# Four weight blocks of an attention-plus-MLP kernel, loaded and split in another place

## The chip, the cores and the metric

The kernel runs on one core of a Trainium2 chip. The metric is the device time of one execution in microseconds, the median of several runs. The core's engines are TensorE (PE, matmuls into the accumulators, PSUM), VectorE (DVE), ScalarE (ACT), GpSimd (POOL) and SyncE (SP), which here issues nearly all the DMA transfers. Each engine takes its instructions strictly in the order in which the program has them, and waits where one of them needs data or a buffer that isn't there.

## The reference

Causal attention with a decay bias over 4 batches of 8 heads, 576 positions and 64 dimensions per head, and behind it two MLPs over the 2304 tokens (512 to 2048 to 512), the first with a leaky ReLU, the second with a softplus.

```
scores = scale * q @ k.T
cum = cumsum(max(s, 0))
scores = where(causal, -1e9, scores + min(-(cum_i - cum_j), 0))
attn = exp(scores - max) / (sum + 1e-9)
x = (attn @ v) rearranged to [2304, 512]
x = leaky(x @ w_in) @ w_out          # first MLP
out = softplus(x @ w2_in) @ w2_out   # second MLP
```

## The kernel before

**Number format.** The matmuls of the MLPs get their operands as pairs of a high and a low part; a product is three matmuls (high by high, high by low, low by high). The weights come from memory in 64-bit words, so each block (512 KB, either an "i" block of w_in or an "o" block of w_out for 128 hidden units) is loaded raw by `load_w` (lines 86 to 96) and then split by `split_w` (98 to 134): two reads of the raw buffer on ScalarE (L105, L106), three steps on VectorE (`clamp` L111, `shift` L114, `sign` L117), an `add` on GpSimd (L120), `high` on ScalarE (L124, which writes wih or woh) and `low` on GpSimd (L130, which writes wil or wol). The two reads are written down at once; the other six steps are put off with `later` by a number of ticks that the call gives (`at`), and `tick` writes down what is due. The order in which the Python code writes the instructions down is the order on each engine: there is no scheduler behind it. A raw buffer is free again when `sign` has read it.

**Attention.** 16 pairs of heads (`NP`), each of four score units, so 64 steps of the loop in `attention` and three more that drain it (step n 0 to 66). The score and transpose matmuls of a step are interleaved with ScalarE's exponentials, VectorE's maxima and GpSimd's scaling (L306). A step has two ticks.

**Units of the first MLP beside it.** A batch that the attention has finished (`ready`) gives 16 units for the first group of four hidden blocks (`G` = 4): an h unit (`Fill.h`) is twelve matmuls of 288 columns and then, each a tick later, gf (ScalarE, L518), gh (ScalarE, L523) and gl (GpSimd, L528); an o unit (`Fill.o`) is twelve matmuls that use the gh and gl of four h units, three for each, in the order gh, gl, gh, and then a copy on ScalarE (L543) and a store of 144 KB on SyncE (L544). `Fill.run` takes one unit per step. Its accumulators rotate over five banks at the end.

**The loads.** `Fill.step` starts a block's load at the steps in `self.loads`, through the single rawi buffer and two rawo buffers, and its split three steps later: the first group's eight blocks from steps 0 to 25, and then four blocks of the second group (4i, 4o, 5i, 5o) at steps 30, 35, 40 and 45, into tiles of a second weight pool with two buffers (`wpool2`).

**Leftover units and main loop.** When the attention is done, seven units are left, three h and four o; a loop runs one of them and a tick per turn (lines 558 to 560). In two turns of it no unit is ready, since the o units need the last gl; TensorE has nothing between, so its order is h, h, h, o, o, o, o. Then come new raw buffers, the loads of the stored part results into `acc` (L567), and the main loop: per step twelve h matmuls (L143), act1 (L605 and others), and the out matmuls (L651) of three steps before. Its `plan` loads and splits the second group's other blocks and all later ones.

Of the kernel before, what the change touches and what calls it, by code (L numbers as in the profile page):

```python
# [19 lines left out]
G = 4  # L20
# [10 lines left out]
def attn_moe_moe(ctx, tc, q, k, v, s, w1i, w1o, w2i, w2o, out):  # L31
# [18 lines left out]
    def pool(name, bufs=1, **kw):  # L50
        return tc.tile_pool(name=name, bufs=bufs, **kw)
# [14 lines left out]
    def later(n, fn, *args):  # L66
        todo.setdefault(clock[0] + n, []).append((fn, args))

    def tick():
        clock[0] += 1  # L70
        for fn, args in todo.pop(clock[0], ()):
            fn(*args)
# [7 lines left out]


    wt, wio = {}, {}
    wpools = [ctx.enter_context(pool(f"wpool{n}", bufs=n)) for n in (G, 2)]
    wio["tmp"] = ctx.enter_context(pool("wtmp", bufs=2))

    def load_w(layer, f, nm, place=None):
        w = ((w1i, w1o), (w2i, w2o))[layer]["io".index(nm)].bitcast(I32)
        raw = (place or wio[nm]).tile([P, 2 * DM], I32, tag="raw", name="raw" + nm)
        if nm == "i":
            nc.sync.dma_start(  # L90
                raw.rearrange("p (k f) -> p k f", k=KD),
                w[:, 2 * f * P:2 * (f + 1) * P].rearrange("(k p) f -> p k f", p=P),
            )
        else:
            nc.sync.dma_start(raw, w[f * P:(f + 1) * P, :])
        wt[layer, f, nm, "raw"] = raw.rearrange("p (e t) -> p e t", t=2)

    def split_w(layer, f, nm, at):

        raw = wt.pop((layer, f, nm, "raw"))  # L100
        L, Hw = raw[:, :, 0], raw[:, :, 1]
        m = wio["tmp"].tile([P, DM], I32, tag="wm", name="wm")
        t = wio["tmp"].tile([P, DM], I32, tag="wt", name="wt")
        wp = wpools[0 if (layer * NF + f) % 6 < 4 else 1]
        nc.scalar.activation(m.bitcast(F32), Hw.bitcast(F32), AF.Abs)  # L105
        nc.scalar.activation(t, L.bitcast(U32), AF.Copy, scale=2.0 ** -29)  # L106

        mf = m.bitcast(F32)

        def clamp():  # L110
            nc.vector.tensor_scalar(mf, mf, D_MIN, D_MAX, op0=ALU.max, op1=ALU.min)  # L111

        def shift():
            nc.vector.tensor_scalar(m, m, 3, 0x3FFFFFFF, op0=ALU.logical_shift_left, op1=ALU.bitwise_and)  # L114

        def sign():
            nc.vector.scalar_tensor_tensor(m, Hw, -0x40000000, m, op0=ALU.bitwise_and, op1=ALU.bitwise_or)  # L117

        def add():
            nc.gpsimd.tensor_tensor(m, m, t, op=ALU.add)  # L120

        def high():
            hi = wp.tile([P, DM], F32R, tag=f"w{nm}h", name=f"w{nm}h")
            nc.scalar.activation(hi, m.bitcast(F32), AF.Copy)  # L124
            wt[layer, f, nm] = [hi]

        def low():
            lo = wp.tile([P, DM], F32R, tag=f"w{nm}l", name=f"w{nm}l")
            hi = wt[layer, f, nm][0]
            nc.gpsimd.tensor_tensor(lo, m.bitcast(F32), hi.bitcast(F32), op=ALU.subtract)  # L130
            wt[layer, f, nm].append(lo)

        for n, fn in zip(at, (clamp, shift, sign, add, high, low)):
            later(n, fn)
# [317 lines left out]
    class Fill:  # L452
        def __init__(self, ps):
            self.ps = ps
            self.units = []
            new = lambda nm, bufs=1: self.stack.enter_context(pool(nm, bufs, side="right"))
            self.stack = ExitStack()
            wio["i"] = new("rawi")
            with_o = pool("rawo", 2, side="right")
            wio["o"] = with_o.__enter__()  # L460

            blocks = [(f, nm) for nm in "io" for f in range(G)] + [(G + f, nm) for f in range(2) for nm in "io"]
            self.loads = dict(zip((0, 2, 5, 8, 11, 15, 20, 25, 30, 35, 40, 45), zip(blocks, "ioooo" + "i" * 7)))

            def begin():

                with_o.__exit__(None, None, None)
                self.gpool, self.tpool = new("gpoolA", G + 1), new("tpoolA", 2)

            self.begin = begin  # L470
# [77 lines left out]
    with pool("psA", bufs=2, space=PSUM) as psA:  # L548
        fills = []

        def make():
            fills.append(Fill(psA))
            return fills[0]

        with pool("att") as att:
            attention(att, psA, make)
        fill = fills[0]
        while fill.units or todo:
            fill.run()
            tick()  # L560
        fill.stack.close()

    for nm in "io":
        wio[nm] = ctx.enter_context(pool("raw" + nm))
    acc = ctx.enter_context(pool("accpool")).tile([P, KD, NT], F32, tag="acc", name="acc")
    for c in range(2 * (B - 1)):
        nc.sync.dma_start(acc[:, :, c * CW:(c + 1) * CW], part[c])  # L567
# [106 lines left out]
    for gi, (layer, g) in enumerate(groups[1:]):  # L674
        a, z = start[groups[gi]], start[layer, g]
        when = [a + 2, a + 5, a + 8, a + 11, z - 3, z, z - 1, z + 2]
        for j, n in enumerate(when):
            if gi == 0 and j < 4:
                continue
            f, nm = divmod(j, 2)  # L680
            w = (layer, g * G + f, "io"[nm])
# [65 lines left out]
```

## Time and profile before

| | |
|---|---|
| runs | 1022.63, 1022.64 and 1021.40 us, median 1022.63 |
| profiled execution | 1022.12 us, of it 1020.20 us span from the first to the last instruction |
| busy, share of the span | PE 97%, DVE 50%, ACT 53%, POOL 55% |
| TensorE's granted clock | 0.997 of 2.4 GHz as a mean |
| stretch with the four splits and the rest of the attention, 112.82 to 263.10 | PE busy 149.55 of 150.28 us |
| leftover units, 263.10 to 275.90 | PE 11.72, ACT 4.63, POOL 2.40, DVE 0.00 us busy of 12.80 |
| first MLP from there, 275.90 to 628.00 | PE busy 349.54 of 352.10 us |
| second MLP, 628.00 to 1020.20 | PE busy 382.67 of 392.20 us |

Times in the rows count from the span's start. "Busy" adds up the durations of an engine's instructions without counting overlap twice. A row of the timeline gives, in brackets, how long the engine was idle before it and what ended that wait.

### The profile page before, as it was taken

The page shows a single profiled execution, that of the slowest core. Times are in us where ns is not written, and L with a number is a line of the kernel's source. Part 1 is how long each engine was busy: PE and PEld are TensorE (multiplying, and loading weights), DVE is VectorE, ACT ScalarE, POOL GpSimd, SP SyncE. Part 2 cuts the span into 40 slices and gives each one's busy share as a digit, 9 for nine tenths or more (in the row PEclk, how much of TensorE's full clock was granted, in tenths as well). Part 3 has the DMA queues.
Part 4 walks back from the last instruction along what each step waited for, and adds up shares of the span by engine and source line. Part 5 has one row for each costly group of instructions (what it writes and reads, how often), then busy time and mean ns, then how long its engine had stood idle before and what let it go on. Part 6 is the DMA issues. An engine that isn't in the chain of part 4 may idle for free.

```text
span 1020.2 us, 15105 instructions
## 1 busy us (share of the span) xinstructions
PE 992.0 (97%) x5498; PEld 812.4 (80%) x5498; DVE 506.3 (50%) x1133; ACT 536.8 (53%) x1152; POOL 559.2 (55%) x565
## 2 busy tenths in 40 slices
PE   7889999999999999999999998999999999999998
PEld 4667788888998888888888887888778877888886
DVE  6886665554021312321244158547575767576443
ACT  4877676656355333432444365666645554565452
POOL 6757455434156335533553356667766676667453
PEclk9999999999999999999999999999999999999999
DMA  5422333210252002100220021101210121010202
GB/s 172 135 97 67 113 106 101 93 59 25 73 205 76 22 1 83 63 21 1 83 62 22 16 68 41 42 2 45 80 42 1 42 82 42 1 42 21 83 22 83
DMA packets 38518, 62.04 MB, mean 61 GB/s; under 512 B 2932, under 2 KB 25972, under 8 KB 38444
## 3 DMA queue, kind: packets, MB, share of 16 engines
q1 hardware_dynamic: 38204, 60.74, 18.2%
q8 instruction: 44, 0.72, 0.3%
q10 hardware_dynamic: 240, 0.33, 0.1%
q14 instruction: 30, 0.25, 0.1%
HBM read 52.65 MB, written 8.40 MB: 60 GB/s over the span
## 4 chain that ended last, share of the span: by engine, by line
PE 73%; POOL 10%; DVE 8%; issue 6%; ACT 3%; DMA 0%; DVEq 0%; POOLq 0%; ACTq 0%
PE ps_h L143 30%; PE ps_out L651 27%; PE pt_v L354 4%; PE ps_o L539 4%; PE pt_s L262 4%; POOL t L619 3%; PE pt_t L323 3%; POOL gl L150 2%; POOL wm L120 2%; DVE wm L114 2%; PE pt_s L252 2%; ACT sc L295 1%; DVE wm L111 1%; DVE wm L117 1%; POOL wil L130 1%
## 5 line engine op out<-in xcount | busy, mean ns | idle before, releaser
L150 POOL TENSOR_TENSOR gl<-gf,gh 128x512 fp32r<-128x512 f32 (+2 forms) x148 | 178.3, 1206 | 258.9 <-ACT gh L149 243.4
L143 PE MATMUL ps_h<-xh,wih 128*128 128x512 f32 (+2 forms) x688 | 246.5, 358 | 1.1 <-ACT o L543 0.6
L143 PE MATMUL ps_h<-xl,wih 128*128 128x512 f32 (+2 forms) x688 | 244.7, 356 | 0.0
L143 PE MATMUL ps_h<-xh,wil 128*128 128x512 f32 (+2 forms) x688 | 243.9, 354 | 0.0
L143 PEld LDWEIGHTS ps_h<-xh,wih 128*128 128x128 f32 x688 | 129.4, 188 | 21.5 <-ACT o L543 0.8
L306 POOL TENSOR_SCALAR sc<-sc,st 128x512 f32<-128x512 f32 (+4 forms) x160 | 88.1, 562 | 103.8 <-DVE st L302 61.3
L143 PEld LDWEIGHTS ps_h<-xl,wih 128*128 128x128 f32 x688 | 129.4, 188 | 19.0
L143 PEld LDWEIGHTS ps_h<-xh,wil 128*128 128x128 f32 x688 | 129.4, 188 | 18.5
L662 DVE TENSOR_TENSOR acc<-ps_out,acc 128x512 f32<-128x512 f32 (+1 forms) x114 | 67.7, 655 | 129.1 <-PE ps_out L651 129.1
L149 ACT ACTIVATE gh<-gf 128x512 fp32r<-128x512 f32 (+2 forms) x148 | 85.3, 576 | 82.7 <-DVE gf L624 81.8
L605 ACT ACTIVATE gf<-ps_h 128x512 f32<-128x512 f32 (+2 forms) x68 | 36.7, 539 | 172.1 <-PE ps_h L143 168.2
L651 PE MATMUL ps_out<-woh,gh 128*128 128x512 f32 x288 | 116.2, 403 | 5.8 <-ACT gh L149 3.2
L624 DVE TENSOR_TENSOR gf<-gf,t 128x512 f32<-128x512 f32 (+1 forms) x80 | 56.0, 700 | 127.0 <-POOL t L619 127.0
L111 DVE TENSOR_SCALAR wm<-wm 128x512 f32<-128x512 f32 x64 | 42.1, 658 | 147.3 <-ACT wm L105 140.3
L651 PE MATMUL ps_out<-wol,gh 128*128 128x512 f32 x288 | 115.0, 399 | 0.0
L295 ACT ACTIVATE sc<-sc,st 128x512 f32<-128x512 f32 (+2 forms) x144 | 83.3, 581 | 42.9 <-DVE st L286 22.0
L120 POOL TENSOR_TENSOR wm<-wm,wt 128x512 int32<-128x512 int32 x64 | 88.1, 1377 | 28.0 <-DVE wm L117 28.0
L619 POOL TENSOR_TENSOR t<-e,t 128x512 f32<-128x512 f32 (+1 forms) x80 | 98.3, 1228 | 0.0
L651 PE MATMUL ps_out<-gh,woh 128*128 128x512 f32 (+2 forms) x272 | 97.1, 365 | 0.0
L651 PE MATMUL ps_out<-gh,wol 128*128 128x512 f32 (+2 forms) x272 | 96.6, 364 | 0.0
L281 DVE CUSTOM_DVE_ANT_0 sc<-pt_s,mask 128x512 f32<-128x512 f32 (+2 forms) x144 | 66.7, 480 | 57.2 <-PE pt_t L323 46.1
L651 PE MATMUL ps_out<-woh,gl 128*128 128x512 f32 x288 | 80.6, 397 | 1.2 <-POOL gl L150 1.1
(93 smaller groups left out, 1729.2 us busy)
## 6 DMA issues: line engine op xcount, KB each, us to landing
rawi<-in_moe_w_in SPq DMA_DIRECT2D x32, 512.0 KB
rawo<-in_moe_w_out SPq DMA_DIRECT2D x32, 512.0 KB
V<-in_v SPq DMA_DIRECT2D x16, 320.0 KB
Q<-in_q SPq DMA_DIRECT2D x15, 320.0 KB
K<-in_k SPq DMA_DIRECT2D x16, 288.0 KB
out<-acc SPq DMA_DIRECT2D x18, 256.0 KB
part<-o SPq DMA_DIRECT2D x24, 144.0 KB
acc<-part SPq DMA_DIRECT2D x6, 576.0 KB
```

The source lines that it names most:

```text
L111: nc.vector.tensor_scalar(mf, mf, D_MIN, D_MAX, op0=ALU.max, op1=ALU.min)
L120: nc.gpsimd.tensor_tensor(m, m, t, op=ALU.add)
L143: nc.tensor.matmul(ps, a, b, start=n == 0, stop=n == 3 * KD - 1)
L149: nc.scalar.activation(gh, gf, AF.Copy)
L150: nc.gpsimd.tensor_tensor(gl, gf, gh.bitcast(F32), op=ALU.subtract)
L281: nc.vector.tensor_tensor_reduce(out=self.sc[:, j, c], in0=self.ps[j][:, c], in1=m, scale=-scale, scalar=3.0e38, op0=ALU.add, op1=ALU.min, ...
L295: nc.scalar.activation(x, x, AF.Exp, scale=-1.0, bias=self.stat(0, e), accum_out=self.stat(1, e))
L306: nc.gpsimd.tensor_scalar(x, x, self.stat(2, e), 1.0, op0=ALU.mult, op1=ALU.mult)
L619: nc.gpsimd.tensor_tensor(t, e, t, op=ALU.subtract)
L624: nc.vector.tensor_tensor(gf, gf, t, op=ALU.add)
L651: nc.tensor.matmul(ps, a, b, start=f == 0 and m == 0, stop=f == G - 1 and m == 2)
L662: nc.vector.tensor_tensor(d, o, d, op=ALU.add)
```

## The change

The four blocks 4i, 4o, 5i and 5o leave the list of the attention. The pool for their split tiles and one raw buffer each for i and o blocks are opened only when the attention's tiles have been given up, so they take that room. The loop over the leftover units now loads 4i and 4o in its turn 0, before that turn's unit, and 5i and 5o in turn 5; it writes the reads of 4i down in turn 2, of 4o in turn 3, of 5i in turn 7 and of 5o in turn 8, and the other six steps of a split 1, 1, 2, 2, 3 and 4 ticks later instead of 1 to 6.

```diff
-    wpools = [ctx.enter_context(pool(f"wpool{n}", bufs=n)) for n in (G, 2)]
+    wpools = [ctx.enter_context(pool("wpool", bufs=G))]
...
-            blocks = [(f, nm) for nm in "io" for f in range(G)] + [(G + f, nm) for f in range(2) for nm in "io"]
-            self.loads = dict(zip((0, 2, 5, 8, 11, 15, 20, 25, 30, 35, 40, 45), zip(blocks, "ioooo" + "i" * 7)))
+            blocks = [(f, nm) for nm in "io" for f in range(G)]
+            self.loads = dict(zip((0, 2, 5, 8, 11, 15, 20, 25), zip(blocks, "ioooo" + "i" * 3)))
...
+        wpools.append(ctx.enter_context(pool("wpool2", bufs=2)))
+        for nm in "io":
+            wio[nm] = ctx.enter_context(pool("raw" + nm))
+        blocks = [(0, G + f, nm) for f in range(2) for nm in "io"]
         fill = fills[0]
+        n = 0
         while fill.units or todo:
+            for j, w in enumerate(blocks):
+                if n == 5 * (j // 2):
+                    load_w(*w)
+                if n == 5 * (j // 2) + 2 + j % 2:
+                    split_w(*w, (1, 1, 2, 2, 3, 4))
             fill.run()
             tick()
+            n += 1
         fill.stack.close()
 
-    for nm in "io":
-        wio[nm] = ctx.enter_context(pool("raw" + nm))
```

TensorE's instructions stand in the same order in both kernels. On ScalarE the leftover units stood in a row before, three pairs of gf and gh and then the four copies of the o units:

```order
L518 ACTIVATE gf_3410<-ps_h_3396 128x288
L523 ACTIVATE gh_3425<-gf_3410 128x288
L518 ACTIVATE gf_3427<-ps_h_3412 128x288
L523 ACTIVATE gh_3444<-gf_3427 128x288
L518 ACTIVATE gf_3446<-ps_h_3429 128x288
L523 ACTIVATE gh_3450<-gf_3446 128x288
L543 ACTIVATE o_3467<-ps_o_3454 128x288
L543 ACTIVATE o_3483<-ps_o_3470 128x288
L543 ACTIVATE o_3499<-ps_o_3486 128x288
L543 ACTIVATE o_3515<-ps_o_3502 128x288
```

From the second unit's gf on, the same place now reads as follows:

```order
L518 ACTIVATE gf_3381<-ps_h_3366 128x288
L105 ACTIVATE wm_3383<-rawi_3346 128x512
L106 ACTIVATE wt_3384<-rawi_3346 128x512
L523 ACTIVATE gh_3402<-gf_3381 128x288
L518 ACTIVATE gf_3406<-ps_h_3387 128x288
L105 ACTIVATE wm_3408<-rawo_3348 128x512
L106 ACTIVATE wt_3409<-rawo_3348 128x512
L523 ACTIVATE gh_3416<-gf_3406 128x288
L124 ACTIVATE wih_3420<-wm_3383 128x512
L124 ACTIVATE woh_3445<-wm_3408 128x512
L543 ACTIVATE o_3447<-ps_o_3430 128x288
L543 ACTIVATE o_3465<-ps_o_3450 128x288
```

The reads of 4i stand between the second unit's gf and gh, those of 4o between the third's, and the highs of both ahead of the first copy.

GpSimd's last rows ahead of the main loop were the three gl of the leftover h units, and behind them the main loop's own (L150):

```order
L528 TENSOR_TENSOR gl_3442<-gf_3410,gh_3425 128x288
L528 TENSOR_TENSOR gl_3448<-gf_3427,gh_3444 128x288
L528 TENSOR_TENSOR gl_3452<-gf_3446,gh_3450 128x288
L150 TENSOR_TENSOR gl_3579<-gf_3563,gh_3578 128x288
L150 TENSOR_TENSOR gl_3598<-gf_3582,gh_3597 128x288
L150 TENSOR_TENSOR gl_3617<-gf_3601,gh_3616 128x288
```

Now, from the first of these three gl to the main loop's first:

```order
L528 TENSOR_TENSOR gl_3400<-gf_3364,gh_3379 128x288
L120 TENSOR_TENSOR wm_3383<-wm_3383,wt_3384 128x512
L528 TENSOR_TENSOR gl_3414<-gf_3381,gh_3402 128x288
L120 TENSOR_TENSOR wm_3408<-wm_3408,wt_3409 128x512
L528 TENSOR_TENSOR gl_3424<-gf_3406,gh_3416 128x288
L130 TENSOR_TENSOR wil_3443<-wm_3383,wih_3420 128x512
L130 TENSOR_TENSOR wol_3463<-wm_3408,woh_3445 128x512
L120 TENSOR_TENSOR wm_3468<-wm_3468,wt_3469 128x512
L120 TENSOR_TENSOR wm_3490<-wm_3490,wt_3491 128x512
L130 TENSOR_TENSOR wil_3518<-wm_3468,wih_3514 128x512
L130 TENSOR_TENSOR wol_3522<-wm_3490,woh_3520 128x512
L150 TENSOR_TENSOR gl_3579<-gf_3563,gh_3578 128x288
```

The add of 4i stands ahead of the second gl, the add of 4o ahead of the third, and both lows and the whole second pair ahead of the main loop's first gl.

SyncE's queue at the end of the attention, from the last load of V, had nine stores, the six loads into acc and the main loop's first loads:

```order
L212 DMA V_92<-in_v 128x640
L544 DMA part<-o 128x288 x9
L567 DMA acc<-part 128x4x288 x6
L90 DMA rawi<-in_moe_w_in 128x4x256 x2
L95 DMA rawo<-in_moe_w_out 128x1024 x2
```

The same queue now, again from the last load of V on:

```order
L212 DMA V_89<-in_v 128x640
L544 DMA part<-o 128x288 x5
L90 DMA rawi<-in_moe_w_in 128x4x256
L95 DMA rawo<-in_moe_w_out 128x1024
L90 DMA rawi<-in_moe_w_in 128x4x256
L95 DMA rawo<-in_moe_w_out 128x1024
L544 DMA part<-o 128x288 x4
L577 DMA acc<-part 128x4x288 x6
L90 DMA rawi<-in_moe_w_in 128x4x256 x2
L95 DMA rawo<-in_moe_w_out 128x1024 x2
```

The first pair of loads stands behind the fifth store, the second pair right behind the first, and the four stores of the last o units behind both.

## Rows read from the trace of the kernel before

**Rows 1.** Windows of three attention pairs: busy us and count per engine, granted clock, DMA.
```profile
162.76:179.85 17.09, 17.09 (x142) 14.25 (x140) 10.52 (x38) 12.10 (x34) 10.80 (x16) 1.00 0.28 88
179.85:197.02 17.17, 17.17 (x141) 14.31 (x139) 10.07 (x38) 11.83 (x33) 8.31 (x14) 1.00 0.24 81
197.02:214.20 17.18, 17.18 (x141) 14.33 (x140) 8.51 (x35) 10.52 (x30) 7.92 (x14) 1.00 0.22 70
```

**Rows 2.** Timeline, GpSimd, 110 to 200: start, duration, engine, line, operation, out<-in.
```profile
130.38 1.28 POOL L120 TENSOR_TENSOR wm<-wm,wt 128x512 int32<-128x512 int32 x1
...
193.53 1.29 POOL L120 TENSOR_TENSOR wm<-wm,wt 128x512 int32<-128x512 int32 x1
```

**Rows 3.** One tile, the split's wm: shortest/median/longest ns, first and last start.
```profile
L111 DVE TENSOR_SCALAR wm<-wm x64: 415/427/1519, 20.9 to 927.0; 128x512 f32<-128x512 f32 x64
L114 DVE TENSOR_SCALAR wm<-wm x64: 406/428/1416, 22.8 to 928.5; 128x512 int32<-128x512 int32 x64
L120 POOL TENSOR_TENSOR wm<-wm,wt x64: 1268/1292/1739, 26.1 to 930.7; 128x512 int32<-128x512 int32 x64
...
L117 DVE SCALAR_TENSOR_TENSOR wm<-rawi,wm x32: 677/693/1666, 23.8 to 911.2; 128x512 int32<-128x512 int32 x32
...
L130 POOL TENSOR_TENSOR wil<-wm,wih x32: 1280/1294/1747, 29.4 to 914.4; 128x512 fp32r<-128x512 f32 x32
```

**Rows 4.** Timeline around the leftover units, rows of SP, ACT, POOL and PE.
```profile
263.79 0.32 SPq L544 DMA_DIRECT2D part<-o  x1
...
267.00 0.45 ACT L523 ACTIVATE gh<-gf 128x288 fp32r<-128x288 f32 x1
...
267.90 0.30 PE L539 MATMUL ps_o<-gh,woh 128*128 128x288 f32 x1
...
268.16 0.41 ACT L518 ACTIVATE gf<-ps_h 128x288 f32<-128x288 f32 x1 [0.71 <-PE ps_h L143]
...
268.61 0.44 ACT L523 ACTIVATE gh<-gf 128x288 fp32r<-128x288 f32 x1
...
269.18 0.80 POOL L528 TENSOR_TENSOR gl<-gf,gh 128x288 fp32r<-128x288 f32 x1 [0.80 <-POOL gl L528]
...
270.03 0.40 PE L539 MATMUL ps_o<-gl,woh 128*128 128x288 f32 x1 [0.53 <-POOL gl L528]
...
275.90 0.40 PE L143 MATMUL ps_h<-xh,wih 128*128 128x288 f32 x1 [0.55 <-ACT o L543]
...
283.38 0.69 PE L651 MATMUL ps_out<-gl,woh 128*128 128x288 f32 x4
```

**Rows 5.** Timeline 293 to 299: two loads, a split's reads; one DMA window behind.
```profile
293.10 0.38 SPq L90 DMA_DIRECT2D rawi<-in_moe_w_in  x1
...
293.53 0.50 SPq L95 DMA_DIRECT2D rawo<-in_moe_w_out  x1
...
296.75 0.67 ACT L105 ACTIVATE wm<-rawi 128x512 f32<-128x512 f32 x1 [0.51 <-DMA rawi<-in_moe_w_in]
...
297.87 0.44 ACT L149 ACTIVATE gh<-gf 128x288 fp32r<-128x288 f32 x1
...
297.10:298.10 1.00, 1.00 (x6) 0.81 (x5) 0.61 (x2) 1.00 (x3) 0.65 (x1) 1.00 0.14 53
```

**Rows 6.** Timeline 610 to 625, VectorE and GpSimd.
```profile
614.77 1.30 POOL L150 TENSOR_TENSOR gl<-gf,gh 128x512 fp32r<-128x512 f32 x1 [4.65 <-ACT gh L149]
...
614.88 1.47 DVE L111 TENSOR_SCALAR wm<-wm 128x512 f32<-128x512 f32 x1
...
616.02 1.48 POOL L619 TENSOR_TENSOR t<-e,t 128x512 f32<-128x512 f32 x1
```

**Rows 7.** TensorE's wait at 628 in its timeline, and two windows behind it.
```profile
628.01 0.75 PE L651 MATMUL ps_out<-woh,gh 128*128 128x512 f32 x1 [2.57 <-ACT gh L149]
...
628.00:630.00 2.00, 1.99 (x5) 1.61 (x6) 0.23 (x1) 1.70 (x3) 1.97 (x2) 0.52 0.00 0
630.00:632.00 2.00, 2.00 (x8) 1.55 (x7) 1.42 (x3) 0.69 (x2) 0.55 (x1) 0.62 0.00 0
```

## The prediction, made before the changed kernel was run

> **What bounds the kernel now.** I first cut the span at the two places that the change touches: the attention pairs in which the four blocks are split now, and the seven leftover units. The table by windows [rows 1] has one attention pair per row, from one pair's first score matmul to the next one's. TensorE is busy for the whole of each row, so in this stretch nothing but TensorE sets the pace. What the reader should look at next is which pairs hold a split. GpSimd's add (L120) stands once per block; of the four that move, one in each of four pairs in a row, [rows 2] shows the first, at 130.38, and the last, at 193.53. The pairs from 162.76 and from 179.85 hold one each, and take 17.09 and 17.17 us. The pair from 197.02 has only the last subtraction of the last block, and takes 17.18 us [rows 1].
>
> The second place is the stretch of the leftover units: three h units, four o units, then the main loop at 275.90. Its timeline [rows 4] shows a chain of three engines with little slack: the second h unit's gh on ScalarE at 267.00, the third's gf and gh at 268.16 and 268.61, the third gl on GpSimd at 269.18, and then TensorE, which already waits 0.53 us for that gl and goes on at 270.03. Whatever delays this gl delays TensorE one for one.
>
> **What is taken out of the attention.** Four loads and four splits leave it. Per block that is two ScalarE reads (1.12 us together, from 296.75 to 297.87 in [rows 5]), three VectorE steps (L111 and L114 at 0.43, L117 at 0.69 us), and two GpSimd passes of 1.29 us [rows 3]. All of it lies beside a TensorE that has no idle time, so I cost the removal at nothing. Bounds: 17.18 less 17.09 us is 0.09 us per pair in the wrong direction for a gain; over four pairs the change is worth between -0.4 and +0.4 us. I take 0.
>
> **What is put beside the leftover units, step by step.** TensorE's order does not change. What changes is what stands ahead of the chain on the other three engines.
>
> 1. *SyncE.* The last store before these units is issued at 263.79 and takes 0.32 us [rows 4]. The two loads stand right behind it, 0.43 us apart as in [rows 5] (293.10 and 293.53). So they go out at 264.15 and 264.6. The nearest row for how long one takes: issued at 293.10, its reader on ScalarE, which waited for that DMA, starts at 296.75 [rows 5], 3.65 us later. The two together had stopped moving bytes within the window 297.10 to 298.10 [rows 5]. So the i block can be read at 267.80, the o block by about 269.2.
>
> 2. *ScalarE.* The i block's two reads stand ahead of the second h unit's gh. That gh would have run at 267.00; it now waits for the DMA until 267.80 and for two reads, and runs at 268.92. The third unit's gf follows at about 269.35; then the o block's two reads, at 269.8 (the load is there by then), and the third gh at 270.9 instead of 268.61.
>
> 3. *VectorE and GpSimd.* On GpSimd the i block's add now stands ahead of the second gl, and the o block's add ahead of the third. The add of the i block needs three VectorE steps behind the read that ends at 268.47: 0.43 + 0.43 + 0.69 and 0.1 between them, 270.1. So it runs from 270.15 to 271.45. The o block's read ends at 270.47, and its first VectorE step falls into that add. What then happens is in [rows 6]: an L111 that began at 614.88, 0.11 us after a GpSimd pass, lasted 1.47 us and ended 0.28 us after that pass had ended; the next GpSimd pass took 1.48 us. The two engines take turns. With turns: L111 ends at 271.73, the second gl at 272.45, L114 at 272.73, L117 at 273.45, the o block's add runs from 273.5 to 274.8, and the third gl from 274.8 to 275.6. TensorE goes on at 275.65 where it went on at 270.03: **+5.6 us**. Without turns the same chain gives the o block's add from 272.25 to 273.55 and the gl's end at 274.35: +4.4. Loads that cost nothing would take off another 0.8 (267.80 back to 267.00): +3.6, which is the lower bound, since the order on GpSimd alone costs that much. I take 5.6, because the L111 row is the same instruction beside the same kind of pass.
>
> 4. *TensorE's clock.* The only wait in this trace that comes near is the one before 628.01: 2.57 us idle, and then the granted clock is 0.52 in the next 2 us and 0.62 in the 2 us behind them [rows 7], that is 1.2 GHz for most of both. The work lost is 2 x 0.48 + 2 x 0.38 = 1.72 us. The waits of about half a microsecond at 270.03 and 275.90 [rows 4] were followed by no fall. In the new kernel the first o unit, which begins at 267.90 with a matmul every 0.13 us [rows 4], comes to the second gh with its seventh, at 268.7; TensorE would wait there to 269.4, from 269.5 to 272.5 for the second gl, and from about 273.0 to 275.65 for the third: two waits of 2.6 us or more, with half a microsecond of work between them. I take one such fall: **+1.7 us**. Bounds: 0, and two such stretches, 3.4.
> The Trainium skill, page "TensorE: Matmul & The Clock Gate", section "HAM oscillation — how this bites in real kernels", says that a wait for data between two bursts of matmuls puts the clock back, so that the next burst starts cold; it speaks against this change, and the row at 628.01 agrees with it. By that rule the sum has the 1.7 us in it, and without it the sum ends at 5.6.
>
> 5. *The second pair of blocks.* Its loads wait on SyncE for the first pair's L117, which frees the buffer: 270.1 and 273.45, so the data is there before ScalarE comes to it behind the second o unit's copy. The stores of the o units stand behind these loads and are not held. Call the main loop's start T. The last read of the second pair ends at about T - 0.9, its add on GpSimd at T + 3.2 at worst (turns again), its last subtraction at T + 5.7, and the main loop's first gl at T + 6.5. In the trace before, T is 275.90, and TensorE first uses such a gl at 283.38, T + 7.5 [rows 4]. So 0.9 us of slack is left, and I cost this at 0; if that cover goes, it costs what goes over, up to about 1.5 us.
>
> 6. *Behind that.* The loads of part results into acc, and the next blocks' loads, keep their places behind the stores and so move with T. TensorE leads from there on; nothing gives the time back.
>
> **Sum.** 0 + 5.6 + 1.7 = 7.3 us. The profiled execution took 1022.12 us (1020.20 of it span); that makes 1029.4. The median of the runs shown is 0.51 above the profiled one, which makes **1029.9 us**. Differences under 0.2% (2.0 us) can't be told from no change here.
>
> **The rivals.**
>
> *The clock holds at 2.4 GHz.* For it: waits broken by a few matmuls are not in the trace. Against it: the one wait of that size in the trace, before 628.01, was followed by the fall. Time: 1022.63 + 5.6 = 1028.2, or 1027.0 where the engines don't take turns (4.4).
>
> *The second pair stalls too.* If the second pair's add or a store lands later than in step 5, ScalarE's first gf of the main loop or GpSimd's first gl misses its 0.9 us of slack, and TensorE waits again, with perhaps a second stretch at 1.2 GHz. Price: 1 to 2.6 us more, 1030.9 to 1032.5. It decides from a first gl later than T + 7.5.
>
> *The attention gets shorter and pays for it: not slower.* Mechanism: a split delays the score chain (VectorE's maxima, ScalarE's exponentials, GpSimd's scaling) and so TensorE's transposes. To be no slower, each of the four blocks taken out must return 7.3 / 4 = 1.8 us to TensorE. It decides from pairs of 15.4 us instead of 17.17. Price if it held in full: 1022.6 or a little below. Against it: pairs with a split are no longer than the one without [rows 1], and TensorE has no idle time in them to give back.
>
> **How the numbers follow.** Forecast, 1029.9 with its own range of 1029 to 1030.9: 0.60. Clock holds: 0.22. Second pair stalls: 0.13. Attention pays: 0.05, of which 0.02 ends faster by over 0.2% and 0.03 within it. The range goes from 1026.5 (the lower bound of step 3 with a little over) to 1032.5 (second stall with a second stretch); it leaves out the last case and the ends of the others. Slower by over 0.2% holds in all but the last case: 0.95.
>
> **What would show it.** Step 1: ScalarE's L105 idle for DMA rawi near 267. Steps 2 and 3: TensorE's o units waiting 2 us or more for gl, twice, before 276, and L120 on GpSimd between the gl's; an L111 of about 1.3 us. Step 4: a granted clock near 0.5 for some 3 us in the windows from 272 to 282. Step 5: the main loop's first matmul near 283.2, with no wait of its own behind it. Attention: pairs still 17.1 us. What would make it wrong: pairs clearly shorter than 17.0, or a third gl that ends before 272.

## The result, and the profile after

The changed kernel takes 1029.90 us (median of 4 runs, 1029.02 to 1030.26), the kernel before 1022.49 (4 runs, 1021.40 to 1022.64). The ratio is 1.0074, 95% interval 1.0056 to 1.0091: slower, by 7.4 us. The profiled execution took 1030.26 us, 1028.4 of it span, against 1022.12 and 1020.20 before.

The windows of the same three attention pairs, columns as in [rows 1], cut at their own first score matmuls:

```profile
163.08:180.17 17.09, 17.09 (x141) 14.24 (x139) 8.53 (x35) 10.77 (x31) 7.42 (x14) 1.00 0.17 58
180.17:197.35 17.18, 17.18 (x142) 14.33 (x140) 8.20 (x35) 10.44 (x30) 6.73 (x13) 1.00 0.26 83
197.35:214.53 17.18, 17.18 (x142) 14.33 (x140) 8.50 (x35) 10.52 (x30) 6.68 (x13) 1.00 0.21 68
```

The splits are gone from them (GpSimd's busy time in the first pair is 7.42 us, where [rows 1] had 10.80), and the pairs take what they took: 17.09, 17.18 and 17.18 us. These pairs begin 0.33 us later than before, where nothing of the change has run yet but the attention without its splits; I take that offset for one of the single execution, because over the eleven profiles of this study the fourteenth pair begins anywhere between 196.29 and 197.65, and in two profiles of the same changed kernel at 197.35 and 197.63. So times around the leftover units are best read from the fourteenth pair's first score matmul, which begins at 197.02 before and at 197.35 after.

Now the leftover units. The next two fences are the timeline of ScalarE and of GpSimd and VectorE, the answer to [rows 4]:

```profile
266.88 0.41 ACT L518 ACTIVATE gf<-ps_h 128x288 f32<-128x288 f32 x1 [0.71 <-PE ps_h L143]
268.45 0.67 ACT L105 ACTIVATE wm<-rawi 128x512 f32<-128x512 f32 x1 [1.16 <-DMA rawi<-in_moe_w_in]
269.02 0.65 ACT L106 ACTIVATE wt<-rawi 128x512 int32<-128x512 uint32 x1
269.58 0.43 ACT L523 ACTIVATE gh<-gf 128x288 fp32r<-128x288 f32 x1
269.91 0.39 ACT L518 ACTIVATE gf<-ps_h 128x288 f32<-128x288 f32 x1
270.20 0.66 ACT L105 ACTIVATE wm<-rawo 128x512 f32<-128x512 f32 x1
270.77 0.66 ACT L106 ACTIVATE wt<-rawo 128x512 int32<-128x512 uint32 x1
271.33 0.43 ACT L523 ACTIVATE gh<-gf 128x288 fp32r<-128x288 f32 x1
```

```profile
270.89 0.43 DVE L111 TENSOR_SCALAR wm<-wm 128x512 f32<-128x512 f32 x1
...
270.96 1.48 POOL L120 TENSOR_TENSOR wm<-wm,wt 128x512 int32<-128x512 int32 x1 [3.86 <-ACT wm L105]
...
271.35 1.37 DVE L114 TENSOR_SCALAR wm<-wm 128x512 int32<-128x512 int32 x1
...
272.40 0.98 POOL L528 TENSOR_TENSOR gl<-gf,gh 128x288 fp32r<-128x288 f32 x1
...
272.76 1.17 DVE L117 SCALAR_TENSOR_TENSOR wm<-rawo,wm 128x512 int32<-128x512 int32 x1
...
274.07 1.26 POOL L120 TENSOR_TENSOR wm<-wm,wt 128x512 int32<-128x512 int32 x1 [0.69 <-DVE wm L117]
...
275.29 0.80 POOL L528 TENSOR_TENSOR gl<-gf,gh 128x288 fp32r<-128x288 f32 x1
```

ScalarE stands still 1.16 us for the load of block 4i, then reads both blocks between the gf and gh of the second and third unit. Behind that, GpSimd's add, VectorE's steps and GpSimd's gl hold each other up: L114 takes 1.37 us instead of 0.43, the add 1.48 instead of 1.28. The last gl ends at 276.09. TensorE's waits in this stretch, from its own timeline:

```profile
270.06 0.40 PE L539 MATMUL ps_o<-gh,woh 128*128 128x288 f32 x1 [0.87 <-ACT gh L523]
...
273.43 0.40 PE L539 MATMUL ps_o<-gl,woh 128*128 128x288 f32 x1 [2.97 <-POOL gl L528]
...
276.14 0.61 PE L539 MATMUL ps_o<-gl,woh 128*128 128x288 f32 x1 [1.94 <-POOL gl L528]
...
284.03 0.40 PE L143 MATMUL ps_h<-xh,wih 128*128 128x288 f32 x1 [0.55 <-ACT o L543]
```

Before, the same timeline had one wait of 0.53 us for gl and one of 0.55 ahead of the main loop [rows 4]. Counted from the fourteenth pair, TensorE goes on from its last gl at 276.14 - 197.35 = 78.79 instead of 270.03 - 197.02 = 73.01, which is 5.78 us later. From there to the main loop it takes 284.03 - 276.14 = 7.89 us instead of 275.90 - 270.03 = 5.87, another 2.02. The reason stands in the windows of 2 us (the last three columns are the granted clock, the DMA share and GB/s):

```profile
272.00:274.00 2.00, 0.57 (x3) 0.43 (x3) 1.89 (x2) 0.63 (x1) 1.38 (x2) 0.96 0.82 261
274.00:276.00 2.00, 0.20 (x1) 0.00 (x0) 0.00 (x0) 0.63 (x1) 1.93 (x2) 0.50 0.52 101
276.00:278.00 2.00, 1.86 (x8) 1.87 (x9) 0.00 (x0) 0.41 (x1) 2.00 (x3) 0.50 0.40 162
278.00:280.00 2.00, 2.00 (x10) 2.00 (x10) 0.00 (x0) 0.10 (x1) 0.56 (x1) 0.50 0.22 74
280.00:282.00 2.00, 2.00 (x15) 2.00 (x14) 1.03 (x3) 1.47 (x4) 0.00 (x0) 0.83 0.21 74
```

The clock is granted at 0.50, 1.2 GHz, through the second of TensorE's long waits and for 4.5 us behind it, while the o units run; smaller windows put its fall at about 273.85, in the short piece of work between the two long waits. From the main loop's start to the end of the span both kernels take the same: 1028.4 - 284.03 = 744.4 and 1020.2 - 275.9 = 744.3 us. So the span's 8.2 us are 0.33 (the offset at the start), 5.78, 2.02 and 0.07. The medians differ by 7.4 us, and the two profiled executions by 8.1: that of the change is the slowest of its runs, 1030.26, and that of before lies below its median, at 1022.12.

### The profile page after: what moved, and what is told of

It is laid out like the page before. It is cut to its first block, busy times and chain, and to the rows that moved or that the text cites. A ratio compares the mean times of both kernels' runs of the same rounds, so it can differ in the third digit from the quotient of the medians.

```text
span 1028.4 us, 15118 instructions
## 1 busy us (share of the span) xinstructions
PE 994.7 (97%) x5498; PEld 814.4 (79%) x5498; DVE 509.8 (50%) x1133; ACT 537.6 (52%) x1152; POOL 558.5 (54%) x565
## 4 chain that ended last, share of the span: by engine, by line
PE 73%; POOL 8%; DVE 8%; issue 5%; ACT 4%; DMA 1%; DVEq 0%; POOLq 0%; SPq 0%; ACTq 0%
PE ps_h L143 29%; PE ps_out L661 27%; PE pt_v L354 4%; PE ps_o L539 4%; PE pt_s L262 4%; PE pt_t L323 3%; POOL t L629 3%; POOL gl L150 2%; POOL wm L120 2%; PE pt_s L252 2%; DVE wm L114 2%; ACT sc L295 1%; DVE wm L111 1%; DVE wm L117 1%; DVE sc L281 1%
## 5 line engine op out<-in xcount | busy, mean ns | idle before, releaser
L150 POOL TENSOR_TENSOR gl<-gf,gh 128x512 fp32r<-128x512 f32 (+2 forms) x148 | 179.1, 1212 | 247.6 <-ACT gh L149 228.8
L111 DVE TENSOR_SCALAR wm<-wm 128x512 f32<-128x512 f32 x64 | 43.9, 685 | 142.2 <-ACT wm L105 142.0
```

The source lines that it names most:

```text
L150: nc.gpsimd.tensor_tensor(gl, gf, gh.bitcast(F32), op=ALU.subtract)
```

## The experiments

Two theories stood against each other, and a third about the clock. The first: the order is the whole cost, because reads, adds and loads stand ahead of a chain that TensorE waits for. The second: the amount of work beside so few units is the cost (with what VectorE and GpSimd take from each other), or part of it is paid back by a shorter attention. In the table, "main loop" is when the main loop's first matmul begins, in us from the fourteenth pair's first one, read from each run's profile.

| kernel | ratio to before (95%) | median, and of the kernel before beside it, us | main loop | lowest clock in the leftover units |
|---|---|---|---|---|
| before | | 1022.49 | 78.88 | 1.00 |
| the change | 1.0074 (1.0056 to 1.0091) | 1029.90, 1022.49 | 86.68 | 0.50 |
| no split of the four | 0.9996 (0.9987 to 1.0005) | 1021.83, 1022.38 | 78.86 | 1.00 |
| only the first pair moved | 1.0074 (1.0060 to 1.0088) | 1029.37, 1022.38 | 86.41 | 0.50 |
| only the second pair moved | 0.9998 (0.9989 to 1.0007) | 1021.87, 1022.38 | 78.88 | 1.00 |
| adds behind the gl | 1.0038 (1.0026 to 1.0050) | 1025.48, 1021.72 | 82.99 | 0.50 |
| splits behind the gl | 1.0020 (1.0011 to 1.0029) | 1024.38, 1022.38 | 79.71 | 1.00 |
| splits behind, mended | 1.0007 (0.9998 to 1.0016) | 1022.60, 1021.95 | 78.88 | 1.00 |
| matmuls in the wait | 1.0061 (1.0049 to 1.0074) | 1028.24, 1021.72 | 84.96 | 1.00 |
| the change, again | 1.0075 (1.0062 to 1.0087) | 1029.89, 1021.95 | 86.97 | 0.50 |
| matmuls in the wait, again | 1.0062 (1.0049 to 1.0074) | 1028.44, 1021.95 | 84.84 | 1.00 |

### Is the attention worth anything without the splits?

```diff
-            for j, w in enumerate(blocks):
+            for j, (layer, f, nm) in enumerate(blocks):
                 if n == 5 * (j // 2):
-                    load_w(*w)
-                if n == 5 * (j // 2) + 2 + j % 2:
-                    split_w(*w, (1, 1, 2, 2, 3, 4))
+                    wt[layer, f, nm] = [wpools[1].tile([P, DM], F32R, tag=f"w{nm}{e}", name=f"w{nm}{e}") for e in "hl"]
+                    for e, t in enumerate(wt[layer, f, nm]):
+                        move(t, wt[0, f - G, nm][e])
```

> This is the changed kernel with the four blocks 4i, 4o, 5i, 5o not loaded and not split at all: in the turns in which they would be loaded, their split tiles are filled by DMA copies of the first group's split tiles, with no work on ScalarE, VectorE or GpSimd. So the attention is without the four splits and the leftover units are without them too. If taking the splits out of the attention is worth nothing and everything lost is lost beside the leftover units, the time is that of the kernel before, 1022.5 us, within 0.6. If the attention is shortened by it (the rival: the new place costs more than the 7.4 us that were measured, and the attention pays part of it back), the time falls below the kernel before by what it pays, 1 to 4 us: 1018.5 to 1021.5.

Measured: 0.9996 of the kernel before (0.9987 to 1.0005), 1021.83 us beside 1022.38 (0.07 us under the range expected), and TensorE's waits beside the leftover units are those of before:

```profile
269.60 0.40 PE L539 MATMUL ps_o<-gl,woh 128*128 128x288 f32 x1 [0.52 <-POOL gl L528]
...
275.47 0.40 PE L143 MATMUL ps_h<-xh,wih 128*128 128x288 f32 x1 [0.55 <-ACT o L543]
```

The main loop begins 275.47 - 196.61 = 78.86 us behind the fourteenth pair, as before to 0.02 us. Taking the four splits away altogether gives nothing that can be measured: what the attention stage gave up was worth nothing, and the new pools and their place cost nothing. All of the loss is made by the loads and splits in their new place.

### Which pair makes it?

One pair of blocks stays in the attention, the other goes where the change has it: 4i and 4o loaded in turn 0 and read in turns 2 and 3, or 5i and 5o read in turns 7 and 8. These two are loaded in turn 0 here, not in turn 5.

```diff
-    wpools = [ctx.enter_context(pool("wpool", bufs=G))]
+    wpools = [ctx.enter_context(pool(f"wpool{n}", bufs=n)) for n in (G, 2)]
...
-            blocks = [(f, nm) for nm in "io" for f in range(G)]
-            self.loads = dict(zip((0, 2, 5, 8, 11, 15, 20, 25), zip(blocks, "ioooo" + "i" * 3)))
+            blocks = [(f, nm) for nm in "io" for f in range(G)] + [(5, nm) for nm in "io"]
+            self.loads = dict(zip((0, 2, 5, 8, 11, 15, 20, 25, 30, 35), zip(blocks, "ioooo" + "i" * 5)))
...
-        wpools.append(ctx.enter_context(pool("wpool2", bufs=2)))
...
-        blocks = [(0, G + f, nm) for f in range(2) for nm in "io"]
+        blocks = [(0, 4, nm) for nm in "io"]
```

The second kernel has 4 and 5 the other way round, loads in turn 0 and reads in turns 7 and 8.

> The first pair 4i, 4o stays where the change puts it; the second pair 5i, 5o is loaded and split beside the attention as in the kernel before. If the second pair is covered (step 5 of the prediction), the whole loss stays: 1029.5 to 1030.5 us. If the loss goes with the amount of work, half of it is left: about 1026 us.

> The first pair is loaded and split beside the attention as in the kernel before; the second pair is loaded in turn 0 of the leftover units and split in turns 7 and 8, where the change has it. If the second pair is covered, the time is that of the kernel before, 1022.5 to 1023.5 us. If the loss goes with the amount of work, about 1026 us.

Measured: 1.0074 for the first pair alone and 0.9998 for the second alone. The medians, 1029.37 and 1021.87 us, lie 0.13 and 0.63 us under the ranges expected, but far from the 1026 of the other theory. The loss does not go with the amount of work: the second pair, the same work, is free, and the first pair alone costs all of it. TensorE's waits with the first pair alone:

```profile
269.52 0.40 PE L539 MATMUL ps_o<-gh,woh 128*128 128x288 f32 x1 [1.00 <-ACT gh L523]
...
272.89 0.61 PE L539 MATMUL ps_o<-gl,woh 128*128 128x288 f32 x1 [2.97 <-POOL gl L528]
...
275.60 0.61 PE L539 MATMUL ps_o<-gl,woh 128*128 128x288 f32 x1 [1.62 <-POOL gl L528]
```

They are close to those of the changed kernel: 1.00, 2.97 and 1.62 us for gh, gl and gl, where that had 0.87, 2.97 and 1.94.

### Is it the order of the adds, or of the reads?

```diff
-                    split_w(*w, (1, 1, 2, 2, 3, 4))
+                    split_w(*w, ((1, 1, 2, 4, 5, 6), (1, 1, 2, 3, 4, 5), (1, 1, 2, 2, 3, 4), (1, 1, 2, 2, 3, 4))[j])
```

> The changed kernel with one difference: the first pair's adds on GpSimd (and the steps behind them) are put off by one or two more turns, so that they stand behind the third gl; the reads still stand ahead of the second and third gh on ScalarE. If order on GpSimd is the larger share of the 5.8 us chain, TensorE goes on when the third gh (271.3 + 0.4) and its gl (0.8 to 1.0) are done, near 272.8 instead of 276.1: 1026.5 us with the stretch at 1.2 GHz, 1024.5 without. If the place of the adds doesn't matter (the loads and reads alone set the chain), the time stays at 1029.9 us.

Measured: 1.0038 (1.0026 to 1.0050), 1025.48 beside 1021.72. TensorE's timeline, and one window of 2 us:

```profile
269.99 0.40 PE L539 MATMUL ps_o<-gh,woh 128*128 128x288 f32 x1 [0.87 <-ACT gh L523]
...
271.45 0.40 PE L539 MATMUL ps_o<-gl,woh 128*128 128x288 f32 x1 [1.06 <-POOL gl L528]
...
272.84 0.40 PE L539 MATMUL ps_o<-gl,woh 128*128 128x288 f32 x1 [0.70 <-POOL gl L528]
...
280.26 0.40 PE L143 MATMUL ps_h<-xh,wih 128*128 128x288 f32 x1 [0.55 <-ACT o L543]
...
274.00:276.00 2.00, 2.00 (x10) 2.00 (x10) 0.00 (x0) 0.88 (x2) 2.00 (x3) 0.50 0.60 146
```

It goes on from the last gl at 272.84 (75.57 behind the fourteenth pair, against 78.79 with the change and 73.01 before). So of the 5.78 us, 3.2 belong to the adds standing ahead of the gl on GpSimd, and 2.6 to the load and the reads ahead of the gh on ScalarE; these two I did not separate. The clock fell here too, for 1.55 us of loss (280.26 - 272.84 = 7.42 instead of 5.87), although no single wait was longer than 1.06 us. The chain came out as expected (272.8), the time did not: with the stretch at 1.2 GHz 1026.5 us was expected, and 1025.48 was measured, between the two values of the expectation.

### Does anything stay if nothing stands ahead of the chain?

First the reads of the first pair behind the third gh, so that the adds come behind the third gl, and the second pair split in the main loop:

```diff
-                if n == 5 * (j // 2):
+                if n == 7 * (j // 2):
                     load_w(*w)
-                if n == 5 * (j // 2) + 2 + j % 2:
+                if j < 2 and n == 4 + j:
                     split_w(*w, (1, 1, 2, 2, 3, 4))
...
-    plan = {}
+    plan = {n: [(split_w, (*w, (1, 1, 1, 1, 2, 2)))] for n, w in zip((1, 3), blocks[2:])}
```

> All four blocks are loaded beside the leftover units as in the changed kernel, but the first pair's reads stand behind the third h unit's gh (turns 4 and 5), so that its adds on GpSimd stand behind the third gl; the second pair is loaded in turn 7 and split in steps 1 and 3 of the main loop. If the cost is the order (reads ahead of gh, adds ahead of gl), TensorE waits no longer than before for the third gl and the time is 1022.5 to 1023.5 us. If it is the amount of work beside the leftover units, or the turns between VectorE and GpSimd wherever the splits stand, half of the loss or more stays: 1026 us or above.

Measured: 1.0020 (1.0011 to 1.0029), 1024.38 us: a miss, outside the first theory's 1022.5 to 1023.5 and not at the second's 1026. The wait for gl is back at 0.54 us. The timeline shows two others in its place:

```profile
270.66 0.40 PE L539 MATMUL ps_o<-gl,woh 128*128 128x288 f32 x1 [0.54 <-POOL gl L528]
...
276.08 0.63 ACT L124 ACTIVATE woh<-wm 128x512 fp32r<-128x512 f32 x1 [1.51 <-POOL wm L120]
...
277.36 0.40 PE L143 MATMUL ps_h<-xh,wih 128*128 128x288 f32 x1 [1.39 <-ACT o L543]
...
282.70 0.41 ACT L615 ACTIVATE gf<-ps_h 128x288 f32<-128x288 f32 x1 [5.39 <-DMA part<-o]
...
283.17 0.40 PE L143 MATMUL ps_h<-xh,wih 128*128 128x288 f32 x1 [0.80 <-ACT gf L615]
```

SyncE's rows there are these:

```profile
275.04 0.38 SPq L90 DMA_DIRECT2D rawi<-in_moe_w_in  x1
275.54 0.49 SPq L95 DMA_DIRECT2D rawo<-in_moe_w_out  x1
277.04 0.80 SPq L544 DMA_DIRECT2D part<-o  x2
```

ScalarE waits with woh (L124) for GpSimd's second add, and behind woh stand the last two copies of the o units, which the main loop's first matmul needs: 1.39 us instead of 0.55. And the first gf of the main loop waits until 282.70 for a store of an o unit, and that costs TensorE 0.80 us. The second pair's loads, 1 MB, stand ahead of the last two stores, and the late copies hold these stores too; how much of the 0.80 us belongs to which I did not separate. Both are order again, so the next kernel takes both away: the highs behind the last copy, the loads behind the last store. Against the kernel just shown:

```diff
-                if n == 7 * (j // 2):
+                if n == 9 * (j // 2):
...
-                    split_w(*w, (1, 1, 2, 2, 3, 4))
+                    split_w(*w, (1, 1, 2, 2, 6 - j, 7 - j))
```

> The kernel of the second experiment with its two new waits taken away: the first pair's highs on ScalarE stand behind the last o unit's copy instead of between the copies, and the second pair's loads stand behind the last o unit's store on SyncE instead of between the stores. All four blocks are still loaded beside the leftover units, and two of them split there. If order is the whole cost, the time is that of the kernel before, 1022.0 to 1023.0 us, with the main loop beginning 78.9 us behind the start of the fourteenth attention pair, as before. If two splits beside the leftover units cost something wherever they stand, it stays at 1024 us.

Measured: 1.0007 (0.9998 to 1.0016), 1022.60 beside 1021.95.

```profile
270.02 0.40 PE L539 MATMUL ps_o<-gl,woh 128*128 128x288 f32 x1 [0.53 <-POOL gl L528]
...
275.89 0.40 PE L143 MATMUL ps_h<-xh,wih 128*128 128x288 f32 x1 [0.55 <-ACT o L543]
```

TensorE's two waits are 0.53 and 0.55 us, those of before, and the main loop begins 78.88 us behind the fourteenth pair. The first pair's loads stand where the change has them, its reads and adds some rows further back beside the same leftover units, and nothing that can be measured is lost. It gains nothing either, since the attention had nothing to give. The expectation says that all four blocks are loaded beside the leftover units; in the trace SyncE issues the second pair's loads at 276.28 and 276.77, when the main loop has just begun (275.89), and the first pair's highs and lows run there too. So this run shows it for one pair of blocks, and the kernel with only the second pair moved shows it for the other.

### Is the clock a cost of its own?

```diff
+            if n == 3:
+                d = psA.tile([P, 512], F32, tag="a", name="ps_d", bufs=1)[:, :CW]
+                for _ in range(4):
+                    h_mm(d, 0, 0, xh[:, :, :CW], xl[:, :, :CW])
             fill.run()
```

> The changed kernel with 48 matmuls more: four h units' worth of matmuls, 6.4 us at the full clock, into an accumulator bank that nothing reads, between the third h unit and the first o unit, where TensorE waits otherwise. If 2 us of the loss are the stretch at 1.2 GHz behind the wait, the granted clock stays at 1.00, the third gl comes at the same time as in the changed kernel, and the time falls by 2.0 us to 1027.9 although TensorE does more work. If the clock costs nothing of its own (the second pair's chain on ScalarE holds the o units' copies anyway), the time stays at 1029.9 us; if the matmuls hold up the first o unit, it rises.

Measured: 1.0061 (1.0049 to 1.0074), so faster than the change by its median (1028.24), though less than expected (1027.9) and with intervals that overlap. Both kernels again, on one chip:

> The changed kernel itself, as a yardstick on the same chip for the run behind it: 1.0074 of the kernel before.

> The kernel with 48 matmuls more in TensorE's wait, again, now beside the changed kernel on one chip. If the stretch at 1.2 GHz costs 2 us of its own, it is 1.7 to 2.0 us faster than the changed kernel; if the clock costs nothing of its own, the two agree within 0.5 us.

Measured: 1028.44 us against 1029.89, 1.45 us less, ratios 1.0062 (1.0049 to 1.0074) and 1.0075 (1.0062 to 1.0087). That is less than the 1.7 to 2.0 us expected and more than the 0.5. All five times with the matmuls lie below all five of the change, but the nearest two only by 0.05 us (1028.77 and 1028.82), and the intervals still touch; by the times alone the size isn't settled. The traces are plain. The window of 10 us and TensorE's waits, first of the change again, then with the matmuls:

```profile
272.00:282.00 10.00, 6.05 (x27) 5.82 (x28) 2.96 (x4) 3.44 (x7) 6.34 (x6) 0.66 0.40 133
...
276.62 0.61 PE L539 MATMUL ps_o<-gl,woh 128*128 128x288 f32 x1 [2.04 <-POOL gl L528]
...
284.60 0.40 PE L143 MATMUL ps_h<-xh,wih 128*128 128x288 f32 x1 [0.55 <-ACT o L543]
```

```profile
272.00:282.00 10.00, 9.16 (x67) 8.69 (x66) 4.40 (x7) 5.03 (x11) 6.72 (x6) 1.00 0.42 137
...
275.54 0.40 PE L539 MATMUL ps_o<-gl,woh 128*128 128x288 f32 x1 [0.29 <-POOL gl L528]
...
281.41 0.40 PE L143 MATMUL ps_h<-xh,wih 128*128 128x288 f32 x1 [0.55 <-ACT o L543]
```

With the matmuls the last gl is awaited to 275.54 - 196.57 = 78.97 us behind the fourteenth pair, no earlier than in the change (276.62 - 197.63 = 78.99); the granted clock is 1.00 instead of 0.66; and from there to the main loop it takes 5.87 us, exactly what it took before, instead of 7.98. In these two traces the stretch at 1.2 GHz is 2.1 us of the loss, and 48 useless matmuls take it away. They are the slowest of the change's five executions and the fastest of the five with the matmuls; over all five the gain is the 1.45 us of the medians.

## Why the prediction was right, step by step

*The attention* was costed at 0, from pairs with a split that were no longer than one without. Right: the pairs of the changed kernel are the same length, and the kernel without the four splits has the time of the one before.

*SyncE and the load.* 3.65 us from the issue to the reader, from [rows 5]; measured 268.45 - 264.61 = 3.84. The load went out 0.14 us later behind the store than forecast. Together that is 0.33 us late.

*ScalarE.* The third gh was forecast at 270.9, or 271.2 with the offset of 0.33; it came at 271.33.

*VectorE and GpSimd.* The place of the two adds and the turns were right, the detail was not: the row had been L111 caught behind a GpSimd pass; here L111 slipped in ahead of the add at 270.89, the add stretched to 1.48 us, and L114 and L117 were caught (1.37 and 1.17). The chain's end was forecast 5.6 us later than before, and measured 5.78. Without turns the prediction's own sum was 4.4. The second gl was forecast at 272.45 (272.78 with the offset) and ended at 273.38, the third at 275.6 (275.93) and ended at 276.09: the error at the second was largely made up at the third.

*The clock.* One fall, costed at 1.72 us from the stretch behind 628; measured 2.02, and 2.1 in the second profile. The forecast had two waits of 2.6 us or more and the fall behind them; they were 2.97 and 1.94 us, and it came between the two, at about 273.85. By the windows the grant falls short by 2 x (0.04 + 0.50 + 0.50 + 0.50 + 0.17) = 3.4 us, twice the 1.72 of the row, but some of that is time in which TensorE had nothing to do. So the agreement to 0.3 us is partly luck: the prediction's sign was a clock near 0.5 for some 3 us, and it stayed there until 280.6, nearly 7 us, with less work in it. And the row it was priced from is of a stage where, by the last section, the fall took no time at all.

*The second pair* was costed at 0, with 0.9 us of slack. Right: alone it costs nothing. Nor does it stall the changed kernel, whose last subtraction of that pair is this:

```profile
288.11 1.29 POOL L130 TENSOR_TENSOR wol<-wm,woh 128x512 fp32r<-128x512 f32 x1
```

It ends 5.37 us behind the main loop's start at 284.03, where the forecast had 5.7. Of the three rivals none came: the clock did not hold, the second pair did not stall, the attention did not pay.

*The sum* was 7.3 us, and the trace's own is 7.8 (5.78 + 2.02). That the median came out at the forecast 1029.9 to the decimal is chance: in the medians the loss is 7.4, in the two profiled executions 8.1.

## What to carry to other kernels

The splits hid beside a TensorE with no idle time and cost nothing there, so moving them away couldn't gain; ask first whether the stage that work leaves is bound by an engine it uses. In the place it goes to, write down for each engine what now stands ahead of the instruction that the bounding engine waits for: here two reads ahead of each of two gh and an add ahead of each of two gl cost 5.8 us of waiting, and the same reads and adds a few rows further back cost nothing. Look where the highs and the loads of the moved work stand, too: with highs ahead of copies and two loads ahead of stores there were two new waits, and none with both further back. Then see whether the waits bring the clock down: that made the loss 1.5 to 2 us larger here.

## What the runs showed of the hardware

The same wait does not always bring the clock down, and its fall does not always cost. At the step from the first MLP to the second, TensorE waits 2.56 to 2.59 us in every profile; behind it the clock fell in eight of the eleven profiles, that of before among them [rows 7], and did not in three. With only the second pair moved:

```profile
627.27 0.50 PE L660 MATMUL ps_out<-woh,gh 128*128 128x512 f32 x1 [2.56 <-ACT gh L149]
...
630.00:640.00 10.00, 10.00 (x45) 8.14 (x44) 7.54 (x11) 7.85 (x14) 6.12 (x5) 1.00 0.01 2
...
656.10 0.50 PE L660 MATMUL ps_out<-woh,gh 128*128 128x512 f32 x1 [0.54 <-ACT gh L149]
...
657.75 0.50 PE L660 MATMUL ps_out<-woh,gh 128*128 128x512 f32 x1 [0.92 <-ACT acc L669]
```

And the kernel before, at the same place:

```profile
658.46 0.51 PE L651 MATMUL ps_out<-woh,gh 128*128 128x512 f32 x1 [0.17 <-ACT acc L660]
```

With only the second pair moved the clock is 1.00 right behind the wait, and yet the stretch from the main loop to the end takes 1019.5 - 275.17 = 744.3 us, as before: TensorE now waits 0.54 and 0.92 us thirty microseconds later, where it waited 0.17 before. So something other than TensorE sets the pace there; the rows name ScalarE as what it waited for, and what held ScalarE I did not look into. The 1.72 us that the prediction took from [rows 7] were work lost, but not time; beside the leftover units, where TensorE led, such a stretch cost 2.0 to 2.1 us in the traces. Nor does the longest single wait alone tell of a fall: with the adds behind the gl the clock fell after waits of 0.87, 1.06 and 0.70 us. The Trainium skill, page "TensorE: Matmul & The Clock Gate", section "HAM oscillation — how this bites in real kernels", tells of the fall behind a wait for data; these traces agree with the fall in eight of the eleven profiles at this step, and show that its price has to be looked up in the stage where it happens.
